# A recurrent attention block and a top-2 router on one core: buffers, order and banks around the attention stage

## The chip, the core and the metric

The kernel runs on one core of a Trainium2 chip. A core has five engines with queues of their own: TensorE (PE in the profile, with PEld for its weight loads), VectorE (DVE), ScalarE (ACT), GpSimd (POOL) and SyncE (SP), which here only issues transfers. The metric is device time in microseconds for one execution; less is better. Six runs of the kernel before gave 670.69 to 676.27 us, median 673.23 us.

## What is computed

The reference, cut to what matters. First a gated recurrence over 768 tokens for 4 batches and 8 heads of width 48, then a router that sends each of the 3072 tokens to two of eight experts.

```python
for t in range(S):                                   # S = 768
    state = f[:, :, t, :, None] * state + k_t (outer) v_t      # f = sigmoid(f_logit)
    y[:, :, t] = q_t @ state
x = y as rows of 384, one per token                  # 3072 rows
logits = x @ w_gate
noisy = logits + log1p(exp(x @ w_noise)) * noise
top2 = the two largest of noisy; weights = softmax over the two
for e in range(8):
    out[rows of e] += weight * (relu(x[rows of e] @ w1[e]) @ w2[e])
```

## The kernel before

**Stages.** The sequence is cut into chunks of 128 tokens: six per batch, so 24 chunks n = 0 to 23 (batch n % 4, group c = n // 4). The attention is a loop over steps i, in which each stage works on a chunk of its own: the sums of the log-gates run two chunks ahead of the scores, the output one behind, the features two behind. A step therefore holds work of up to six chunks. Within one step the instructions are issued in the order of the `for stage, lag in (...)` line, and `in_order` (L1222) fixes that order on every engine: nothing is reordered later, and an instruction that waits holds up everything behind it on its engine.

**One step, by engine.** TensorE: the transposes `kp` of k (L588, into PSUM bank 0), the state's share of the output `y` (L614), the scores `sc` (L599), the transposes `qp` (bank 3), `kp` (bank 1) and `fp` (bank 0), all three L555, the output `y` (L660), the state's update `ds` in two halves (L633: the first half into bank 2, the second into bank 0), the features `xp` (L670, bank 1). ScalarE: `yT` (L623), the decays `P` and `Q` (L574, L576), `far`, two passes for `f` (L560, L561), `cap`, the copy `dss` of the state's second half (L645), the copy `xs` of the x rows (L675), the copy `kn` (L593). VectorE: the scan `L` (L569), the masked scores `A` (L602), `qP` and `kQ` (L581, L583), `half` (L638), the logits' sums `lg` (L673). GpSimd: the clamp of f two chunks ahead (L549), then `mid` (L648) and the new state `st` (L649), which add and scale what `dss` holds. A state made at chunk n is first read at chunk n + 4.

**Shared results.** `lg` and `xs` read the same bank. The order of tracing decides which goes first, and the second carries a wait for the first. A bank is written again only when its last reader is done: `kp` of L588 waits for `dss` (both use bank 0), `kp` of L555 waits for the last reader of `xp` (bank 1), `xp` for `kQ` (bank 1), `ds` for the last reader of bank 2.

**The router** runs in small pieces between the stages, one group of four chunks at a time. Its last part multiplies counts on TensorE (`rk`, L734 and L735), copies them on ScalarE (`ranks`, L737), turns them into list positions on VectorE (L740 to L745), and appends each token to its experts' lists with 8 indirect transfers from GpSimd per group (`put`, L749). One put is issued for every third slot of the loop, from group 3 on for every slot.

**The weights.** The first two experts' weights are loaded in parts during the last steps (`weights_part`, L868): w1 in three parts of 128 rows, w2 in three parts of 3, 3 and 2 blocks. They are queued on SP, in its order, behind the other loads of the step. Each transfer of that queue also waits for the one eight before it. From then on TensorE works through experts; a load of weights for expert e + 2 (L864, L866) waits in SP's queue for TensorE to be done with expert e.

The last parts of expert 1 stand in SP's queue behind such a load.

Of the kernel before, what the change touches and what calls it, by code (L numbers as in the profile page):

```python
# [10 lines left out]
F32 = mybir.dt.float32  # L11
# [4 lines left out]
AX = mybir.AxisListType  # L16
ALU = mybir.AluOpType
# [314 lines left out]
def kernel(  # L332
# [38 lines left out]
    nc = tc.nc  # L371
    B, H, S, D = q.shape
    N, DM = out.shape
    E = moe_w_gate.shape[1]
    FF = moe_w1.shape[2]
    C = 128
    NCH = S // C
    HP = H // 2
    DP = 64
    KO = DM // 128  # L380
    FO = FF // 128
# [32 lines left out]
    wk = attention.enter_context(tc.tile_pool(name="wk", bufs=2))  # L414
    ps2 = attention.enter_context(tc.tile_pool(name="ps2", bufs=1, space=PSUM))
    turns = [(ps1, 3)]

    def one_bank(name, which=None):
        if which is None and len(turns) == 2 and name.startswith("xgp"):
            pool, which = turns[0]  # L420
        elif which is None or len(turns) > 2:
            turns.append(turns.pop(0))
            pool, which = turns[-1]
        else:
            pool = ps1
            if which == 3 and len(turns) == 2:
                which = 1
        return pool.tile([128, 512], F32, tag=f"bank{which}", name=name)

    def two_banks(name, tag="two"):  # L430
# [64 lines left out]
    XW = 2 * D  # L495
# [129 lines left out]
    def advance(n):  # L625
        c, b = n // B, n % B
        last = c == NCH - 1
        vt = pads["v"][n % RING["v"]]
        ds = [one_bank(f"ds{k}_{n}", 2 - 2 * k) for k in range(1 if last else 2)]
        for hp in range(HP):  # L630
            for k, par in ((0, 0), (1, 1), (0, 1), (1, 0)):
                if k < len(ds):
                    nc.tensor.matmul(ds[k][rows(par), hp * DP:(hp + 1) * DP], lhsT=kn[n][rows(k), 2 * hp + par, :],  # L633
                                     rhs=vt[rows(k), 2 * hp + par, :], start=True, stop=True)
        dsv = [t[:, 0:HP * DP].rearrange("d (a e) -> d a e", e=DP) for t in ds]
        half = wk.tile([128, HP, DP], F32, tag="half", name=f"half_{n}", bufs=3)
        if c:
            nc.vector.tensor_tensor(half, dsv[0], state[b], ALU.add)  # L638
        else:
            nc.vector.tensor_copy(half, dsv[0])  # L640
        before[n] = state[b], half
        if last:
            return
        dss = wk.tile([128, HP, DP], F32, tag="ds", name=f"dss_{n}", bufs=1)
        nc.scalar.copy(dss, dsv[1])  # L645
        new = wk.tile([128, HP, DP], F32, tag=f"st{b}", name=f"st_{n}")
        mid = wk.tile([128, HP, DP], F32, tag="mid", name=f"mid_{n}", bufs=1)
        nc.gpsimd.tensor_tensor(mid, dss, half, ALU.add)  # L648
        nc.gpsimd.tensor_tensor(new, mid, far[:, n, :].unsqueeze(2).broadcast_to((128, HP, DP)), ALU.mult)  # L649
        state[b] = new  # L650
# [15 lines left out]
    def features(n):  # L666
        c, b = n // B, n % B
        xp = one_bank(f"xp_{n}", 1)[:, 0:HP * (XW + 2 * E)].rearrange("t (a w) -> t a w", a=HP)
        for hp in range(HP):
            nc.tensor.matmul(xp[:, hp, :], lhsT=yT[n][:, hp].rearrange("e r t -> e (r t)"), rhs=w_rt[:, hp, :], start=True, stop=True)  # L670
        if b == 0:
            lg[c] = rt.tile([128, B, 2 * E], F32, tag="lg", name=f"lg_{c}", bufs=NCH)
        pace["f"] = nc.vector.tensor_reduce(lg[c][:, b, :], xp[:, :, XW:].rearrange("t a e -> t e a"), axis=AX.X, op=ALU.add)  # L673
        xs = wk.tile([128, HP, XW], F32, tag="xs", name=f"xs_{n}", bufs=3)
        nc.scalar.copy(xs, xp[:, :, 0:XW])  # L675
        xw.append(lambda: nc.sync.dma_start(out=x_rows[n * C:(n + 1) * C, :], in_=xs.rearrange("t a w -> t (a w)")))


    def route(c):
# [50 lines left out]
                                     data1=each.rearrange("t e b -> t (e b)"), initial=0.0, op0=ALU.mult, op1=ALU.add)  # L730
        for _ in range(2 if c == 0 else 5):
            yield from pause()
        rk = one_bank(f"rk_{c}", 3)[:, 0:B * E].rearrange("t (e b) -> t e b", b=B)
        nc.tensor.matmul(rk, lhsT=earlier, rhs=each[:, :, 1:], start=True, stop=False)  # L734
        nc.tensor.matmul(rk, lhsT=ones, rhs=upto[c][:, :, 0:B], start=False, stop=True)  # L735
        ranks = t([E, B], "ranks")
# [29 lines left out]
    def enough():  # L766


        total = one_bank("total_a")[:, 0:E]
        nc.tensor.matmul(total, lhsT=ones, rhs=upto[HALF - 1][:, :, B], start=True, stop=True)  # L770
        lack = rt.tile([1, E], F32, tag="lack", name="lack", bufs=1)
        nc.vector.tensor_scalar(lack, total[0:1, :], 255.5, None, ALU.is_lt)
        nc.vector.tensor_reduce(short, lack, axis=AX.X, op=ALU.max)
        yield

    def plan():


        def t(shape, tag, dtype=F32):
            return rt.tile([128] + shape, dtype, tag=f"{tag}_plan", name=f"{tag}_plan", bufs=1)  # L780

        total = one_bank("total_b")[:, 0:E]
        nc.tensor.matmul(total, lhsT=ones, rhs=upto[NCH - 1][:, :, B], start=True, stop=True)
        full, cnt, ends = t([E, NI], "full"), t([E], "cnt"), t([E], "ends")
        nc.vector.tensor_tensor(full, total.unsqueeze(2).broadcast_to((128, E, NI)),
                                over_of.unsqueeze(1).broadcast_to((128, E, NI)), ALU.is_gt)
        yield
        nc.vector.tensor_reduce(cnt, full, axis=AX.X, op=ALU.add)
        nc.vector.tensor_tensor_scan(ends, data0=ones[:, 0:E], data1=cnt, initial=0.0, op0=ALU.mult, op1=ALU.add)
        step, past, ex, row = t([E], "step"), t([NI, E], "past"), t([NI], "ex"), t([NI], "row")  # L790
        nc.vector.tensor_scalar(step, cnt, -1.0, float(N // QS), ALU.mult, ALU.add)
        yield
        nc.vector.tensor_tensor(past, block.unsqueeze(2).broadcast_to((128, NI, E)),
                                ends.unsqueeze(1).broadcast_to((128, NI, E)), ALU.is_ge)
        yield
        nc.vector.tensor_reduce(ex, past, axis=AX.X, op=ALU.add)
        nc.vector.tensor_tensor(past, past, step.unsqueeze(1).broadcast_to((128, NI, E)), ALU.mult)
        nc.vector.tensor_reduce(row, past, axis=AX.X, op=ALU.add)
        yield
        nc.vector.tensor_tensor(row, row, block, ALU.add)  # L800
        nc.vector.tensor_scalar(row, row, float(3 * 256 // QS), float(E * N // QS), ALU.add, ALU.min)
        nc.vector.tensor_scalar(ex, ex, float(E - 1), None, ALU.min)
        to = top.tile([128, NI, 2], I32, tag="steer", name="steer")
        nc.vector.tensor_scalar(to[:, :, 1], row, float(QS), None, ALU.mult)
        nc.vector.tensor_copy(to[:, :, 0], ex)
        yield
        steer_q.extend(to[0:1, n, :] for n in range(NI))
        nc.vector.tensor_scalar(more, ends[0:1, E - 1:E], NQ + 0.5, None, ALU.is_gt)
        nc.vector.scalar_tensor_tensor(short, in0=ends[0:1, E - 1:E], scalar=NI + 0.5, in1=short, op0=ALU.is_gt, op1=ALU.max)
        yield  # L810
# [56 lines left out]

    def weights_part(k, which, part):  # L868
        if which == 1:
            return nc.sync.dma_start(out=w1[k][:, part], in_=moe_w1[k, part * 128:(part + 1) * 128, :])  # L870
        else:
            few = slice((part * FO + 2) // 3, ((part + 1) * FO + 2) // 3)
            return nc.sync.dma_start(out=w2[k][:, few], in_=moe_w2[k].rearrange("(f p) d -> p f d", p=128)[:, few])

    def turned(p, s):
# [420 lines left out]
    for i in range(-3, NS + 2):  # L1296
        for stage, lag in ((summed, -2), (finish, 2), (decays, -2), (scores, 0), (scaled, -2), (forget, -3),
                           (output, 1), (advance, 0), (features, 2), (upright, -1), (upright_copy, -1)):
            n = i - lag
# [3 lines left out]
            if stage is forget:  # L1303
                clamp(n + 2, nc.gpsimd if n else nc.vector)
            elif stage is scaled:
                load("q", n + 3)
                load("k", n + 3)
                if n < 2:
                    load_router(n)
                    load("v", n + 1)  # L1310
            elif stage is finish:
                while xw:
                    xw.pop(0)()
            elif stage is scores:
                load("v", n + 3)
            elif stage is advance:
                if n in (2, 7, 8, 9, 10, 11):
                    load_router(2 + (2, 7, 8, 9, 10, 11).index(n))
                for bit in {18: (0,), 19: (1,), 20: (2, 3), 21: (4, 5), 22: (6, 7), 23: (8, 9, 10, 11)}.get(n, ()):
                    weight = weights_part(bit // 6, bit // 3 % 2 + 1, bit % 3)  # L1320
                    if n < NS - 2:
                        spaced(weight, "k")
                if n >= NS - 2:
                    zeros(HALF * B // 2)
            elif stage is upright_copy:
                load("f", i + 7)
# [24 lines left out]
        n = i - 2  # L1351
# [83 lines left out]
```

## Time and profile before

| | |
|---|---|
| six runs, median | 673.23 us |
| the profiled execution | 674.02 us |
| its span, first to last instruction | 672.3 us |
| TensorE busy | 637.5 us, 95% |
| VectorE busy | 439.6 us, 65% |
| ScalarE busy | 253.0 us, 38% |
| GpSimd busy | 273.3 us, 41% |
| mean granted TensorE clock | 0.983 |

The span falls into three stretches. Up to about 165 us is the attention with the router between; from there to about 659 us the experts; then some 13 us in which the last results are written. A window row of the profile gives, after the length of the window, the busy time of TensorE, of its weight loads, of VectorE, ScalarE and GpSimd, each with its number of instructions, then the granted clock of TensorE as a share of full speed, the busy share of the 16 DMA engines and what they moved. A row of the view of waits gives who waited for whom, the sum in us, how often, and the longest. A timeline row gives start, length, engine, line and operation; the bracket is the idle time before it and what ended it.

### The profile page before, as it was taken

What the parts mean: (1) busy time and instruction counts of PE and PEld (TensorE: products, weight loads), DVE (VectorE), ACT (ScalarE), POOL (GpSimd) and SP (SyncE); (2) the same over time, 40 slices, a digit from 0 to 9 for tenths busy, and PEclk for the clock granted to TensorE, in tenths of its full rate; (3) what the DMA queues carried; (4) which work ended last, traced back from release to release, by engine and by line L of the source; (5) the groups of instructions that cost most, each with busy time, mean ns of one, the idle gap of its engine ahead of it and who ended that gap; (6) DMA issues with size and microseconds to landing.
All of it is one profiled execution on the core that took longest, in us unless ns stands there. A gap on an engine that the chain in (4) does not pass through costs nothing.

```text
span 672.3 us, 16495 instructions
## 1 busy us (share of the span) xinstructions
PE 637.5 (95%) x6637; PEld 580.5 (86%) x6637; DVE 439.6 (65%) x1041; ACT 253.0 (38%) x597; POOL 273.3 (41%) x304
## 2 busy tenths in 40 slices
PE   6999998899999999999999999999999999999992
PEld 5788887787899999999989898898988989989891
DVE  6668776774446754445666877677876677767761
ACT  5687775662222121212243333333233232233320
POOL 8544798775066632333122424142341332502121
PEclk9999997999999999999999999999999999999997
DMA  9979798767789567662134577375872757702122
GB/s 179 193 167 210 152 193 193 170 180 272 262 246 309 195 170 233 203 175 48 12 68 111 165 271 197 112 210 154 283 188 94 223 164 269 185 25 26 21 25 28
DMA packets 159174, 110.61 MB, mean 165 GB/s; under 512 B 115104, under 2 KB 149408, under 8 KB 159088
## 3 DMA queue, kind: packets, MB, share of 16 engines
q1 hardware_dynamic: 146912, 89.91, 46.4%
q0 software_dynamic: 12176, 19.55, 13.9%
q8 instruction: 54, 0.88, 0.5%
q14 instruction: 32, 0.26, 0.1%
HBM read 88.56 MB, written 21.12 MB: 163 GB/s over the span
## 4 chain that ended last, share of the span: by engine, by line
PE 86%; ACT 4%; DVE 3%; DMA 2%; issue 1%; POOL 1%; SPq 0%; POOLq 0%; DVEq 0%; ACTq 0%
PE y L1039 31%; PE hp L931 13%; PE P L958 6%; PE W L958 4%; PE V L958 4%; PE X L958 4%; PE Z L958 4%; PE xp L670 3%; PE xgp L880 2%; PE qp L555 2%; PE y L660 2%; PE ds L633 1%; PE sc L599 1%; PE y L614 1%; PE kp L588 1%; PE kp L555 1%
## 5 line engine op out<-in xcount | busy, mean ns | idle before, releaser
L1048 POOL DMA_INDIRECT out_dram<-ys,slots x48 | 81.3, 1695 | 210.7 <-ACT ys L1105 155.2
L1039 PE MATMUL y<-qk_all,f_all 128*128 128x192 f32 x576 | 105.5, 327 | 0.0
L1039 PEld LDWEIGHTS y<-qk_all,f_all 128*128 128x128 f32 x576 | 93.5, 190 | 0.5 <-DVE xt L881 0.2
L931 PE MATMUL hp<-xt,w 128*128 128x256 f32 x384 | 86.2, 381 | 0.4 <-ACT kn L593 0.2
L931 PEld LDWEIGHTS hp<-xt,w 128*128 128x128 f32 x384 | 72.0, 190 | 9.9 <-ACT kn L593 0.4
L1039 PE MATMUL y<-w,hs 128*128 128x192 f32 x384 | 71.0, 328 | 1.0 <-DVE mid L1107 1.0
L1039 PEld LDWEIGHTS y<-w,hs 128*128 128x128 f32 x384 | 63.6, 190 | 2.4 <-DVE mid L1107 1.1
L1021 DVE TENSOR_TENSOR f_all<-hs 128x512 f32<-128x512 f32 x48 | 32.4, 689 | 40.4 <-ACT hs L933 34.9
L749 POOL DMA_INDIRECT lists<-entry,sloti x48 | 51.9, 1082 | 14.7 <-issue 8.1
L856 POOL DMA_INDIRECT xg<-x_rows,slots x48 | 50.8, 1058 | 14.5 <-issue 10.5
L933 ACT ACTIVATE hs<-hp 128x512 f32<-128x512 f32 x32 | 19.1, 597 | 73.7 <-PE hp L931 73.7
L1179 POOL DMA_INDIRECT out_dram<-ys_q,slots_q x5 | 8.6, 1716 | 80.4 <-DVE ys_q L1177 80.4
L1105 ACT ACTIVATE ys<-ys,slots 128x384 f32<-128x384 f32 x24 | 14.8, 616 | 66.4 <-DVE ys L1104 64.5
L549 POOL TENSOR_SCALAR f_all<-f_all 128x384 f32<-128x384 f32 x21 | 27.3, 1300 | 26.8 <-DMA f_all<-in_f_logit_dram 14.2
L958 PE MATMUL P<-sides,v_all 128*128 128x256 f32 x128 | 38.1, 379 | 0.0
L881 ACT COPY xt<-xgp 128x384 f32<-128x384 f32 x32 | 15.3, 478 | 57.3 <-PE xgp L880 57.3
L994 ACT ACTIVATE hs<-hs 128x256 f32<-128x256 f32 x32 | 13.4, 418 | 59.0 <-DVE hs L974 59.0
L1039 PE MATMUL y<-qk_all,hs 128*128 128x192 f32 x192 | 35.3, 327 | 0.1
L1039 PE MATMUL y<-w,f_all 128*128 128x192 f32 x192 | 35.1, 326 | 0.0
L958 PE MATMUL X<-xt,w 128*128 128x256 f32 x128 | 32.9, 379 | 0.0
L958 PE MATMUL Z<-xt,v_all 128*128 128x256 f32 x128 | 32.8, 379 | 0.0
L1097 DVE TENSOR_TENSOR ys<-P,y 128x192 f32<-128x192 f32 x24 | 8.5, 354 | 35.8 <-PE y L1039 23.1
(197 smaller groups left out, 1422.5 us busy)
## 6 DMA issues: line engine op xcount, KB each, us to landing
w<-in_moe_w_dram SPq DMA_DIRECT2D x24, 1536.0 KB
w_q<-in_moe_w_dram SPq DMA_DIRECT2D x10, 1536.0 KB
f_all<-in_f_logit_dram SPq DMA_DIRECT2D x24, 192.0 KB
qk_all<-in_q_dram SPq DMA_DIRECT2D x24, 192.0 KB
qk_all<-in_k_dram SPq DMA_DIRECT2D x24, 192.0 KB
v_all<-in_v_dram SPq DMA_DIRECT2D x24, 192.0 KB
x_rows<-xs SPq DMA_DIRECT2D x24, 192.0 KB
out_dram<-zero SPq DMA_DIRECT2D x24, 192.0 KB
```

The source lines that it names most:

```text
L549: engine.tensor_scalar(raw, raw, XMIN, None, ALU.max)
L555: nc.tensor.transpose(p[:, cols(hp)], flat[:, cols(hp)], ident)
L670: nc.tensor.matmul(xp[:, hp, :], lhsT=yT[n][:, hp].rearrange("e r t -> e (r t)"), rhs=w_rt[:, hp, :], start=True, stop=True)
L749: into = nc.gpsimd.indirect_dma_start(out=lists, out_offset=bass.IndirectOffsetOnAxis(ap=sloti[:, r, b:b + 1], axis=0), in_=entry[:, c, b, ...
L856: nc.gpsimd.indirect_dma_start(out=xg[p][:, s, :], out_offset=None, in_=x_rows[0:HALF * B * C] if p < E else x_rows, in_offset=bass.Indire ...
L881: (nc.vector.tensor_copy if p < E else nc.scalar.copy)(xt[p][:, :, s * 128:(s + 1) * 128], xp[:, 0:DM].rearrange("d (k t) -> d k t", k=KO))
L931: nc.tensor.matmul(hp[:, o, :], lhsT=w1[home(k)][:, i, (fo + o) * 128:(fo + o + 1) * 128], rhs=xt[k][:, i, :], start=(i == 0), stop=(i == ...
L933: nc.scalar.activation(hs[:, fo:fo + 2, :], hp, AF.Relu)
L958: nc.tensor.matmul(to, lhsT=x, rhs=y, start=start, stop=stop)
L1021: nc.vector.tensor_tensor(sm[which], x, y, op)
L1039: nc.tensor.matmul(P[name], lhsT=x[:, o, :], rhs=y[:, o, :], start=(o == 0), stop=(o == FH - 1))
L1048: into = nc.gpsimd.indirect_dma_start(out=out, out_offset=bass.IndirectOffsetOnAxis(ap=slots[p][:, s, 2:3], axis=0), in_=ys[s], in_offset= ...
```

## The change

- `dss` (L645) gets three buffers in place of one.
- `xs` (L675) is traced ahead of `lg` (L673): ScalarE's copy reads the bank first.
- `rk` moves from bank 3 to bank 2, the counts `total_a` and `total_b` too.
- The first two experts' weights come in eight parts each in place of six: w1 by quarters of its columns (1 KB pieces of a row in place of 4 KB rows, 384 KB a part), w2 by four equal parts (384 KB a part). They are issued at other steps: expert 0's w1 one part each at chunks 17 to 20, its w2 at 21; expert 1's w1 at 22, its w2 at 23.

Apart from the exchange of `xs` and `lg` in tracing, the order of instructions on TensorE, VectorE, ScalarE and GpSimd is the same; on SP only the weights' parts move.

```diff
@@ one_bank
             pool = ps1
-            if which == 3 and len(turns) == 2:
-                which = 1
@@ advance
-        dss = wk.tile([128, HP, DP], F32, tag="ds", name=f"dss_{n}", bufs=1)
+        dss = wk.tile([128, HP, DP], F32, tag="ds", name=f"dss_{n}", bufs=3)
@@ features
-        pace["f"] = nc.vector.tensor_reduce(lg[c][:, b, :], xp[:, :, XW:].rearrange("t a e -> t e a"), axis=AX.X, op=ALU.add)
         xs = wk.tile([128, HP, XW], F32, tag="xs", name=f"xs_{n}", bufs=3)
         nc.scalar.copy(xs, xp[:, :, 0:XW])
+        pace["f"] = nc.vector.tensor_reduce(lg[c][:, b, :], xp[:, :, XW:].rearrange("t a e -> t e a"), axis=AX.X, op=ALU.add)
@@ route
-        rk = one_bank(f"rk_{c}", 3)[:, 0:B * E].rearrange("t (e b) -> t e b", b=B)
+        rk = one_bank(f"rk_{c}", 2)[:, 0:B * E].rearrange("t (e b) -> t e b", b=B)
@@ enough, plan
-        total = one_bank("total_a")[:, 0:E]
+        total = one_bank("total_a", 2)[:, 0:E]
...
-        total = one_bank("total_b")[:, 0:E]
+        total = one_bank("total_b", 2)[:, 0:E]
@@ weights_part
         if which == 1:
-            return nc.sync.dma_start(out=w1[k][:, part], in_=moe_w1[k, part * 128:(part + 1) * 128, :])
+            few = slice(part * FF // 4, (part + 1) * FF // 4)
+            return nc.sync.dma_start(out=w1[k][:, :, few], in_=moe_w1[k].rearrange("(k p) f -> p k f", p=128)[:, :, few])
         else:
-            few = slice((part * FO + 2) // 3, ((part + 1) * FO + 2) // 3)
+            few = slice(part * FO // 4, (part + 1) * FO // 4)
             return nc.sync.dma_start(out=w2[k][:, few], in_=moe_w2[k].rearrange("(f p) d -> p f d", p=128)[:, few])
@@ the loop, stage advance
-                for bit in {18: (0,), 19: (1,), 20: (2, 3), 21: (4, 5), 22: (6, 7), 23: (8, 9, 10, 11)}.get(n, ()):
-                    weight = weights_part(bit // 6, bit // 3 % 2 + 1, bit % 3)
+                for bit in range(n - 17, n - 16) if 17 <= n < 21 else range(4 * n - 80, 4 * n - 76) if n >= 21 else ():
+                    weight = weights_part(bit // 8, bit // 4 % 2 + 1, bit % 4)
                     if n < NS - 2:
                         spaced(weight, "k")
```

## The prediction

> **What bounds the kernel now.** I read the windows first, to find where TensorE stands still or runs slowly.
>
> ```profile
> 105.00:110.00 5.00, 3.11 (x92) 2.56 (x90) 4.83 (x19) 2.77 (x8) 4.56 (x8) 1.00 0.88 192
> 110.00:115.00 5.00, 3.85 (x58) 3.41 (x59) 0.96 (x3) 3.06 (x7) 4.69 (x7) 0.55 0.94 205
> 115.00:120.00 5.00, 5.00 (x105) 4.87 (x104) 2.77 (x9) 1.92 (x6) 2.00 (x3) 0.77 0.93 203
> ...
> 130.00:135.00 5.00, 2.29 (x36) 1.94 (x40) 2.96 (x16) 1.43 (x4) 4.45 (x7) 0.94 0.74 190
> 135.00:140.00 5.00, 5.00 (x131) 4.65 (x124) 3.52 (x11) 3.57 (x10) 2.72 (x5) 0.72 0.39 83
> ```
>
> From 200 us to 650 us TensorE is busy all the time, so only the attention can give. There two places stand out: TensorE idles for over two microseconds and the clock then falls to half. Next, the view of waits over the whole span says who is late.
>
> ```profile
> ACT xs L675 <- DVE lg L673: 29.8, 21, 4.9
> ...
> ACT dss L645 <- POOL mid L648: 6.9, 4, 3.2
> ```
>
> The same view of TensorE alone, up to 200 us: its longest wait is for that copy `dss`, and two smaller ones belong to the router's `rk`.
>
> ```profile
> PE kp L588 <- ACT dss L645: 6.2, 4, 2.7
> ...
> PE rk L734 <- DVE qP L581: 1.3, 2, 1.0
> PE qp L555 <- ACT ranks L737: 1.2, 1, 1.2
> ```
>
> The timelines show the mechanism: GpSimd is a step behind with puts, `mid` of the last chunk is late, the single `dss` buffer is still being read, and ScalarE, then TensorE, stand behind it.
>
> ```profile
> 109.82 0.87 POOL L648 TENSOR_TENSOR mid<-dss,half 128x256 f32<-128x256 f32 x1
> 110.72 0.37 ACT L645 COPY dss<-ds 128x256 f32<-128x256 f32 x1 [2.87 <-POOL mid L648]
> 111.15 1.12 PE L588 MATMUL kp<-ident,kQ 128*128 128x128 f32 x4 [2.38 <-ACT dss L645]
> 117.13 0.76 PE L660 MATMUL y<-A,v_all 64*64 64x64 f32 x32
> ...
> 133.77 0.66 PE L588 MATMUL kp<-ident,kQ 128*128 128x128 f32 x4 [2.71 <-ACT dss L645]
> 138.24 0.69 PE L660 MATMUL y<-A,v_all 64*64 64x64 f32 x32
> ```
>
> And a clean step, for the margin that the new order of `xs` and `lg` uses:
>
> ```profile
> 37.57 0.23 DVE L673 TENSOR_REDUCE lg<-xp 128x16 f32<-128x64 f32 x1 [0.56 <-PE xp L670]
> 37.71 1.28 DVE L569 TENSOR_TENSOR_SCAN L<-f,cap 128x512 f32<-128x512 f32 x1
> 37.83 0.48 ACT L675 COPY xs<-xp 128x384 f32<-128x384 f32 x1 [0.85 <-DVE lg L673]
> 39.16 0.65 ACT L574 ACTIVATE P<-L 128x512 f32<-128x512 f32 x1
> 40.45 0.68 DVE L583 TENSOR_TENSOR kQ<-kp,Q 128x512 f32<-128x512 f32 x1
> 41.59 1.15 PE L670 MATMUL xp<-w_rt,yT 128*128 128x112 f32 x8
> ```
>
> **Three buffers for `dss`.** The wait for `mid` one chunk back becomes one for three chunks back. GpSimd was one step late in both places, so it is gone.
>
> *First place.* `xp` ends at 108.77; in the undisturbed step `kp` starts 0.17 before the end of `xp` (125.06 against 124.08 + 1.15), so here at 108.60 in place of 111.15: 2.55 us. From `kp` to `y` of L660 the slow clock took 117.13 - 111.15 = 5.98; the undisturbed step takes 127.91 - 125.06 = 2.85, plus 0.56 for the two `rk` (143.82 to 144.38): 3.41, so 2.57 more. Gain 5.1, if nothing else ends later.
>
> *Second place.* `xp` ends at 131.07, `kp` could start at 130.90 in place of 133.77: 2.87. Then 138.24 - 133.77 = 4.47 against 2.85: 1.62. Gain 4.5.
>
> That the slow clock follows from the idling is read from three cases: after 2.66, 2.38 and 2.71 us of idling (`kp` at 14.92, 111.15, 133.77) the windows show 0.50, after the gaps of up to 1.7 us they don't. The Trainium skill speaks against this half of the gain ("TensorE: Matmul & The Clock Gate", "HAM oscillation — how this bites in real kernels"): no idle gaps over some 3.4 us is its rule, so these gaps would not have cost the clock. By it the slow spells have another cause and stay, and 4.2 us of the sum would fall away. I go by the three rows, in which the clock drops at the gap's end.
>
> What is late next: GpSimd's clamp and `st` are still a step behind. The clamp is read two steps later, `st` four chunks later; GpSimd does 2.00 us of work in 115 to 120 and catches up. That cover is a step, some 5.3 us; without it `fp` waits.
>
> **`xs` ahead of `lg`.** ScalarE stops waiting (29.8 us in all), but it mostly waits for TensorE's `kp` right after, so this gains nothing by itself. VectorE now starts `lg` after `xs`: in the clean step at 37.54 + 0.03 + 0.48 + 0.03 = 38.08 in place of 37.57, half a microsecond later. Behind `lg` stand the scan `L`, `A`, `qP`, `kQ`; behind `kQ`, `xp`. `L` would start 0.14 after `lg` and end at 39.50, so `P` moves from 39.16 to 39.5 and `kQ` ends 0.34 later, at 41.47. `xp` starts at 41.59: the margin of 0.46 just covers it. Reading all steps so, it is not covered in three: `xp` at 64.79 starts 0.05 after `kQ` (loss 0.5), at 83.04 it is 0.25 (0.34 lost, since `P` hangs on `L` there), at 150.55 it is 0.11 (0.25). Sum: 1.1 us lost. Bounds: nothing, if ScalarE's lead helps as much; 0.5 for each of the 16 steps from 52 to 150 us, 8 us, if VectorE's routing work leaves no margin. I take 1.1, by the rows.
>
> It also shortens the two gains. In the second place `lg` starts at 131.6, `L` 0.5 later behind a maximum and its index, and the rows' lengths bring `kQ` to 136.0, `xp` to 136.05 against 139.61: 3.6 gained, not 4.5.
>
> **`rk` in bank 2.** Before, `rk` waits for `qP` (bank 3) and the next `qp` for `ranks`. Now `ds` waits for `ranks`. Group 0: `qp` no longer waits (1.17), and `ds` comes 2.2 us later, when `ranks` is long done: 1.1 gained. Groups 1 and 3: `rk` need not wait 0.96 and 0.30, but `ranks` ends at 89.20 and 145.12, where `ds` started at 89.21 and 145.13: nothing gained, nothing lost. Group 2 falls into the first place: `P` starts after `L` at 110.70, `ranks` ends 2.74 later as at 142.38 to 145.12, so at 113.45; TensorE would be at `ds` at 108.60 + 3.41 + 0.75 = 112.76. It waits 0.75: `xp` at 114.1 against 118.52, so 4.4 gained there, not 5.1. Behind the waiting `ds` stand `xp` and the whole next step. `total_a` (119.50) waits for `half` (119.14): nothing. Bounds for all groups: 1.3 gained if ScalarE is early, 3 lost if it is 0.75 late four times.
>
> **The weights.** No engine's work changes; SP issues 16 parts in place of 12, at some 0.45 us each, 1.8 us of its idle time. Expert 0's w2 now comes whole at chunk 21: 1.57 MB from 150.5 on in place of 0.98. At 357 GB/s (window 150 to 155) that takes 4.4 us in place of 2.8; its first reader is VectorE at 158.28, so some 3 us remain for the last bytes to land. If that cover went, VectorE would stand up to 4.85 us without TensorE noticing (its idle time before `A` at 165.34). Expert 1's w1 no longer stands behind the load that waits until 171.74; TensorE reads it at 188.82, so this gains nothing. The pieces shrink to 1 KB; nearest row: w2's 1.5 KB pieces and the zeros moved at 391 GB/s. Value 0; bounds: 0.9 lost (one more stop like the 0.94 us before `sc` at 153.80, where the DMA engines are full), 0.9 gained. The skill ("DMA: Bandwidth & Descriptors", "Measured (HBM→SBUF, 128 partitions, SWDGE, issued from GpSimd)") wants transfers of 1 MiB; by its fit of 2.0 us plus bytes over 436 GB/s, four parts one after another are an estimated 11.6 us, and VectorE would wait until 162, still inside its idle time.
>
> **Sum.** 4.4 + 3.6 + 1.1 - 1.1 = 8.0 us, of 674.0 us in the profiled execution: 666.0. It lies 0.8 above the median of 673.2, so the median should go to 665.2; I say 665.5, as a stop in the full DMA stretch is likelier to grow than to shrink. All experts start earlier by the same amount, and their loads hang on TensorE's progress, so nothing is given back there.
>
> **Rivals.** (a) The clock has another cause. For it: after other gaps, of up to 1.7 us, the clock stayed, so idling doesn't always cost it; against it three long gaps in three. 8.0 - 2.57 - 1.62 = 3.8 us: 669.4. (b) The loop of `xp`, `xs`, `lg`, `L`, `P`, `Q`, `kQ` becomes the bound wherever the router works: 16 steps at 0.5 take back 8 us in place of 1.1, leaving 1.1: 672.1. For it: VectorE is busy 4.83 of 5 us at 105; against it: it was late there for its own sake, `xs` was done before it came to `lg` would be, and the shift is then nothing (`lg` at 103.41, 1.4 after `xp`). (c) Slower: `ds` waits for `ranks` so long that the clock falls. Place: `ds` in groups 1 to 3; price 2.4 us of idling plus 2.1 (mean of 2.57 and 1.62), three times 13.5, against 8.0: 678.7. It decides from 2.4 us of lateness; the rows show 0 and my sum 0.75. That the wait for `mid` isn't what the profile says I hold for unlikely: ScalarE resumes within 0.05 us of its end, twice.
>
> **How the numbers follow.** Forecast 0.73, own range 661.5 to 669.5; (a) 0.08; (b) 0.11; (c) 0.08. Low end: 5.1 + 4.5 + 1.1 + 1.3 = 12 us gained and nothing lost, 661, and 0.5 for the runs' scatter; high end reaches to (b): 672. A change of 0.5% (3.4 us, to 669.9) is about what this measurement can tell from none. Faster: nearly all of the forecast and part of (a): 0.76; within: (b), the rest: 0.16; slower: 0.08.
>
> **What would show it.** After: no row of `dss` waiting for `mid` over 0.5 us; windows from 100 to 140 with the clock at 1.00; `lg` about 0.5 after `xp`; `ds` waiting for `ranks` under 1 us in group 2; `xp` of chunk 17 some 8 us earlier, and the end with it. I am wrong if a slow spell stays without a gap before it (a), if `xp` waits for `kQ` in most steps (b), or if a new gap over 2 us stands before `ds` (c).

## The result and the profile after

| | before | after |
|---|---|---|
| median of all runs beside each other | 672.47 us (51 runs) | 668.77 us (25 runs) |
| ratio, with its 95% interval | | 0.9946 (0.9933 to 0.9959) |
| the profiled execution | 674.02 us | 668.17 us |
| its span | 672.3 us | 666.4 us |
| mean granted TensorE clock | 0.983 | 0.989 |

The change gains 3.6 us, 0.54%. The interval lies wholly below 1, so it is faster, though only just by more than the 0.5% that the prediction named as about what can be told from none. The forecast was 8.0 us. The direction held and the size was under half; at 668.77 us the median still lies inside the prediction's own range of 661.5 to 669.5, 0.7 us from its slow end. The two profiled executions lie further apart than the medians, 5.9 us, since the one of before was 1.6 us slower than its median and the one after 0.6 us faster.

In the changed kernel most lines of the attention are numbered two lower (`ds` L631, `f` L558, `P` L572, `L` L567, `dss` L643, `ranks` L735); `xs` is L672 and `lg` L673. TensorE's view of waits, up to 200 us (who waited for whom, sum in us, times, longest):

```profile
PE ds L631 <- ACT f L558: 6.0, 13, 0.9
PE ds L631 <- ACT ranks L735: 3.9, 3, 1.9
PE kp L586 <- ACT f L558: 2.7, 1, 2.7
PE qp L553 <- DVE qP L579: 1.2, 1, 1.2
...
PE kp L586 <- ACT dss L643: 1.0, 2, 0.5
```

The wait for `dss`, 6.2 us with a longest of 2.7, is down to 1.0 us, and no row of `dss` waiting for `mid` is left. In its place `ds` now waits: for `ranks` 3.9 us where it was nothing, and for `f` 6.0 us, where the same view of before has

```profile
PE ds L633 <- ACT f L560: 1.8, 4, 0.7
```

Not all of this comes from the exchange; the second and third set of experiments tell more.

Of all engines, in the same stretch, the exchange of `xs` and `lg` shows thus:

```profile
ACT xs L672 <- PE xp L668: 19.2, 20, 2.9
DVE lg L673 <- ACT xs L672: 17.7, 22, 1.6
ACT P L572 <- DVE L L567: 14.4, 17, 1.7
```

ScalarE no longer waits for `lg`; VectorE waits for `xs` instead, and then ScalarE for the scan `L`, 14.4 us in 17 waits, where before had 4.0 in 3.

The windows of the two places of before, with the clock in the third column from the end, now run at full speed:

```profile
110.00:115.00 5.00, 3.68 (x138) 3.32 (x133) 3.36 (x11) 3.30 (x10) 4.92 (x7) 1.00 0.89 191
115.00:120.00 5.00, 4.47 (x122) 4.04 (x111) 3.67 (x5) 3.45 (x10) 4.32 (x7) 1.00 0.94 200
...
130.00:135.00 5.00, 4.76 (x106) 4.46 (x106) 4.86 (x12) 2.90 (x7) 4.68 (x7) 1.00 0.78 193
```

Behind them the clock is not full throughout: a period of half clock begins at 139.44 us, told below.

The next table shows where time was won and lost. It gives, at the start of `xp` of some chunks, how much earlier (minus) each trace is than the profiled execution of before. Three of the later experiments stand beside it: `dss` alone is `e9_dss`, the exchange alone `e10_swap`, `dss` and banks `e11_dss_rk`.

| `xp` of chunk | before, us | after | `dss` alone | exchange alone | `dss` and banks |
|---|---|---|---|---|---|
| 0 | 31.03 | -1.81 | -0.35 | -1.76 | -0.50 |
| 3 | 46.79 | -0.60 | -0.52 | -0.55 | -0.67 |
| 6 | 64.79 | -0.21 | -1.52 | -0.89 | -1.77 |
| 7 | 71.80 | -1.57 | -1.53 | -0.48 | -3.13 |
| 13 | 107.62 | -2.06 | -1.27 | -0.22 | -2.71 |
| 14 | 118.52 | -5.90 | -5.19 | -3.08 | -7.41 |
| 16 | 129.92 | -5.47 | -5.36 | -3.11 | -7.27 |
| 17 | 139.61 | -8.76 | -8.62 | -2.53 | -10.54 |
| 19 | 150.55 | -5.74 | -5.67 | -1.55 | -7.51 |
| 23 | 186.63 | -6.08 | -6.31 | -1.88 | -7.98 |

Take the column "after" by its steps. From chunk 13 to 14 it gains 3.8 us, from 16 to 17 3.3: these are the two stops behind `dss`. At chunk 7 it gains 1.4: group 0's `qp` no longer waits for `ranks`. Two losses stand against that: 1.2 us between chunks 0 and 3, where no router works, and 3.0 us between 17 and 19. (The 1.8 us at chunk 0 are no part of the change: before, the clock fell after the gap at 14.9 us; here the same gap, 2.65 us, left it alone. More on this in the last section.) The five steps sum to 3.8 + 3.3 + 1.4 - 1.2 - 3.0 = 4.3 us, and with the 1.8 of chunk 0 they are the 6.1 us at chunk 23. From chunk 20 on nothing changes any more.

**The first loss, a clean step.** The timelines of ScalarE, VectorE and TensorE in the changed kernel (start, length, engine, line, operation, bracket with the idle time before it and its releaser):

```profile
36.09 0.48 ACT L672 COPY xs<-xp 128x384 f32<-128x384 f32 x1 [0.60 <-PE xp L668]
...
36.60 0.23 DVE L673 TENSOR_REDUCE lg<-xp 128x16 f32<-128x64 f32 x1 [1.09 <-ACT xs L672]
36.74 1.49 DVE L567 TENSOR_TENSOR_SCAN L<-f,cap 128x512 f32<-128x512 f32 x1
...
38.27 0.63 ACT L572 ACTIVATE P<-L 128x512 f32<-128x512 f32 x1 [0.67 <-DVE L L567]
...
39.41 0.59 ACT L558 ACTIVATE f<-fp 128x512 f32<-128x512 f32 x1
...
40.05 0.69 PE L631 MATMUL ds<-v_all,kn 64*64 64x64 f32 x30 [0.40 <-ACT f L558]
```

The same place before:

```profile
40.31 0.61 ACT L560 ACTIVATE f<-fp 128x512 f32<-128x512 f32 x1
...
40.97 0.69 PE L633 MATMUL ds<-v_all,kn 64*64 64x64 f32 x30
```

The exchange makes `lg` wait for `xs`, so the scan `L` starts half a microsecond later. ScalarE gets to `P` and stands 0.67 us for `L`. Behind `P` in ScalarE's order are `Q`, `far` and then the first pass of `f`, which reads `fp` in bank 0. The second half of `ds` writes bank 0, so TensorE stands 0.40 us for `f`. Before, `f` ended at 40.92 and `ds` followed without a wait.

**The second loss, group 3 of the router.** The same timelines, a hundred microseconds later:

```profile
133.34 0.19 DVE L673 TENSOR_REDUCE lg<-xp 128x16 f32<-128x64 f32 x1
133.46 1.63 DVE L567 TENSOR_TENSOR_SCAN L<-f,cap 128x512 f32<-128x512 f32 x1
...
135.12 0.63 ACT L572 ACTIVATE P<-L 128x512 f32<-128x512 f32 x1 [1.57 <-DVE L L567]
...
137.65 0.18 ACT L735 COPY ranks<-rk 128x32 f32<-128x32 f32 x1
...
137.88 0.68 PE L631 MATMUL ds<-v_all,kn 64*64 64x64 f32 x16 [1.90 <-ACT ranks L735]
```

VectorE comes late to `lg` because of its routing work. `P` waits 1.57 us for `L`, both passes of `f` and then `ranks` follow, and the first half of `ds`, which now shares bank 2 with `rk`, stands for 1.90 us. After that the clock is at half for a while, though the gap is shorter than all those that cost the clock before. Windows of the changed kernel, cut where the clock changes (last columns: granted clock, DMA share, GB/s):

```profile
136.03:139.44 3.41, 1.56 (x24) 1.50 (x25) 2.23 (x7) 1.73 (x6) 1.50 (x3) 1.00 0.43 97
139.44:142.85 3.41, 3.41 (x60) 2.88 (x60) 1.97 (x4) 2.50 (x5) 2.80 (x3) 0.50 1.05 243
142.85:146.27 3.42, 3.42 (x82) 3.06 (x80) 1.82 (x4) 0.57 (x3) 2.70 (x3) 1.00 0.95 316
```

Half clock for 3.41 us costs up to 1.7 us of work; with the wait of 1.90 that covers the 3.0 us of the table. In another execution of the changed kernel (`e8_after`) a wait of 1.88 us at the same place was not followed by half clock, and 2.0 us were lost between chunks 17 and 19.

### The profile page after: what moved, and what is told of

Read it like the earlier page. It is cut to its first block, busy times and chain, and to the rows that moved or that the text cites. A ratio compares the mean times of both kernels' runs of the same rounds, so it can differ in the third digit from the quotient of the medians.

```text
span 666.4 us, 16496 instructions
## 1 busy us (share of the span) xinstructions
PE 633.9 (95%) x6637; PEld 577.4 (87%) x6637; DVE 441.4 (66%) x1041; ACT 254.7 (38%) x597; POOL 272.0 (41%) x304
## 4 chain that ended last, share of the span: by engine, by line
PE 80%; ACT 5%; DVE 5%; DMA 4%; issue 2%; POOL 2%; SPq 1%; POOLq 0%; DVEq 0%; ACTq 0%
PE y L1038 32%; PE hp L930 13%; PE P L957 7%; PE W L957 4%; PE Z L957 4%; PE V L957 4%; PE X L957 4%; DVE L L567 3%; PE xp L668 3%; PE xgp L879 2%; PE ds L631 1%; ACT f L558 1%; ACT P L572 1%; PE yp_q L1172 1%; PE hp_q L1157 1%
## 5 line engine op out<-in xcount | busy, mean ns | idle before, releaser
L1047 POOL DMA_INDIRECT out_dram<-ys,slots x48 | 79.8, 1663 | 208.7 <-ACT ys L1104 158.2
L547 POOL TENSOR_SCALAR f_all<-f_all 128x384 f32<-128x384 f32 x21 | 24.8, 1181 | 27.8 <-DMA f_all<-in_f_logit_dram 19.9
L567 DVE TENSOR_TENSOR_SCAN L<-f,cap 128x512 f32<-128x512 f32 x24 | 32.2, 1343 | 1.5 <-ACT cap L562 1.5
```

The lines of the kernel that those rows point to most:

```text
L547: engine.tensor_scalar(raw, raw, XMIN, None, ALU.max)
L567: nc.vector.tensor_tensor_scan(L[n], data0=logf[n], data1=cap[n % 2].rearrange("d a t -> d (a t)"), initial=0.0, op0=ALU.add, op1=ALU.min)
L1047: into = nc.gpsimd.indirect_dma_start(out=out, out_offset=bass.IndirectOffsetOnAxis(ap=slots[p][:, s, 2:3], axis=0), in_=ys[s], in_offset= ...
```

## The experiments

Two theories at the start. A: the stops behind `dss` are worth about what the prediction reckoned, and the reordering gave part of it back. B: the stops were covered by other work, and there was little to gain. The kernels of one set ran on one chip; each ratio is against the kernel before in the same set.

**First set: each part alone.** `e1_dss` is the kernel before with `bufs=3`, `e2_swap` with `xs` and `lg` exchanged, `e3_rk` with the ranks and totals in bank 2, `e4_weights` with the weights in eight parts; in each case these lines of the change and no others.

> Before, with three buffers for dss and nothing else. Theory A (the two buffer stops were worth what the prediction says; the other order of xs and lg and the ranks' new bank gave part of it back): both stops and both slow spells go, 5.1 + 4.5 us by the rows of before, less a little that comes up behind them; 7 to 9.5 us faster, ratio 0.986 to 0.990. Theory B (the stops were covered by other work: VectorE's and GpSimd's queues set the pace there once the buffer no longer does): the same 3.6 us as the whole change or less, ratio 0.994 or above.

> Before, with only xs traced ahead of lg. Theory A: P hangs on L in nearly all steps, so both passes of f come later and the second half of ds, which writes f's bank, waits for them: the waits of ds for f grow from 1.8 us (4 times) to about 6 us (13 times); 2 to 4 us slower, ratio 1.003 to 1.006. Theory B: the margins cover it, within 1 us of before, ratio 0.9985 to 1.0015.

> Before, with only the ranks and the totals in bank 2. Theory A: 1.2 us gained in group 0, and ds waits for ranks in groups 1 to 3, 0.7 to 1.9 us each, with a slow spell where it is 1.9: 0 to 3 us slower, ratio 1.000 to 1.005. Theory B: only the group 0 gain counts, ratio 0.998.

> Before, with only the weights in eight parts at the new steps. Both theories: VectorE waits some 2 us for expert 0's w2 and TensorE does not notice: ratio 0.9985 to 1.0015. If the denser transfers stop TensorE's instructions (as in the one stop of 0.94 us that the profile of before puts down to nothing), up to 1 us slower.

Measured: 698.72 us, ratio 1.0033 (1.0006 to 1.0059); 697.96 us, 1.0015 (0.9992 to 1.0039); 698.95 us, 1.0009 (0.9982 to 1.0035); 699.09 us, 1.0028 (1.0007 to 1.005). On this chip the kernel before itself took 697.57 us, some 25 us more than in the runs above. None of the four is faster; `e1_dss` and `e4_weights` are 0.3% slower, with intervals clear of 1. By the numbers B would stand, but the traces show that something else held TensorE up here. TensorE's waits up to 200 us with `dss` in three buffers:

```profile
PE y L614 <- issue: 7.8, 15, 1.1
PE ds L633 <- issue: 7.1, 14, 1.1
```

and a window of it:

```profile
120.00:140.00 20.00, 16.02 (x340) 13.39 (x343) 8.72 (x19) 9.70 (x26) 15.41 (x23) 0.83 0.45 97
```

"issue" means that TensorE waited for nothing that the profile shows. It idled 14.9 us this way ahead of the small matmuls of `y` and `ds`, the clock was at 0.83, and the stretch went slowly whatever the other engines did. The other three traces have such rows too. The four runs say nothing on A or B where these gaps are absent, and the same questions were put again.

**Second set: the change with one part undone.** The kernel before took 670.91 us here. `e8_after` is the changed kernel itself. `e5_no_swap` undoes the exchange alone:

```diff
+        pace["f"] = nc.vector.tensor_reduce(lg[c][:, b, :], ...)
         xs = wk.tile([128, HP, XW], F32, tag="xs", name=f"xs_{n}", bufs=3)
         nc.scalar.copy(xs, xp[:, :, 0:XW])
-        pace["f"] = nc.vector.tensor_reduce(lg[c][:, b, :], ...)
```

`e6_no_rk` puts ranks and totals back where they were before. `e7_dss_rk0` is the kernel before with three buffers for `dss` and `one_bank(f"rk_{c}", 3 if c else 2)`: bank 2 for group 0 only.

> The changed kernel itself, so that all of this call stand beside it on one chip. Theories A and B: ratio 0.993 to 0.996 to before as in the result. Theory C, where the gaps fill the steps: 1.000 to 1.004.

> After, with lg traced ahead of xs again (so: three buffers, ranks in bank 2, eight parts). Theory A (half of the gain was given back by the new order of xs and lg and by the ranks): 2 to 3 us faster than the changed kernel of this call; the waits of ds for f fall from 6.0 us (13 times) to 2 us or less. Theory B (the removed stops were covered by other work): as the changed kernel, within 1 us, whatever the waits of ds say. Theory C (the four runs before this: TensorE there stood 0.3 to 0.5 us at a time before small matmuls of the state without anything to wait for, from about 85 to 180 us, and the step was set by that): where such gaps fill the steps, no edit shows, and all kernels of this call lie within 0.4% of before.

> After, with the ranks in bank 3 and the totals by turns again. Theory A: the waits of ds for ranks (3.9 us, 3 times, and a slow spell behind the one of 1.9) go, the wait of qp for ranks in group 0 (1.2 us) comes back, and rk waits again for qP: 1 to 3 us faster than the changed kernel. Theory B: as the changed kernel. Theory C: within 0.4% of before.

> Before, with three buffers for dss and the ranks in bank 2 for group 0 alone; order of xs and lg, the other banks and the weights as before. Theory A: 9 to 10.5 us faster than before, ratio 0.985 to 0.988, the fastest of this call. Theory B: 0.994. Theory C: within 0.4% of before.

Measured: `e8_after` 667.69 us, 0.995 (0.9926 to 0.9974); `e5_no_swap` 664.3 us, 0.9904 (0.9868 to 0.9939); `e6_no_rk` 671.87 us, 1.0021 (0.9998 to 1.0045); `e7_dss_rk0` 664.53 us, 0.9909 (0.9878 to 0.9941).

The change repeats its gain in this set. Without the exchange it is 3.4 us faster, where A had 2 to 3. The waits of `ds` for `f` fall from 4.7 us (`e8_after`) to 2.8, not to the 2 that A named, and those for `ranks` from 4.0 to 2.8: 3.1 us together, about the gain. So A is right that the exchange gives part back, and the rest of both waits is there without it. `e7_dss_rk0` gains 6.4 us, less than the 9 to 10.5 of A. About the ranks A is wrong. It took their move for one of the steps that gave something back; undone, the kernel is 4.2 us slower, not faster. TensorE's waits in `e6_no_rk`:

```profile
PE ds L633 <- ACT f L560: 5.2, 13, 0.7
PE rk L734 <- DVE qP L581: 3.5, 3, 1.7
```

With the ranks in bank 3 `rk` waits for `qP`, 3.5 us where before had 1.3. The exchange isn't needed for this wait: `e9_dss` below, with the old order, has 3.2 us of it, and `e10_swap`, the exchange without the buffers, only 1.6. The wait of `qp` for `ranks` in group 0 is back as well, 1.5 us, and the trace, like that of the changed kernel, has a period of half clock at 139 us. Without the exchange, bank 2 for all groups (`e5_no_swap`) and for group 0 alone (`e7_dss_rk0`) come to the same. So the new bank is worth 4.2 us beside the exchange and, by the third set, some 0.6 without it. Why so much more is not shown.

**Third set: the parts alone again, and a better order.** The kernel before took 670.75 us. `e9_dss` and `e10_swap` are `e1_dss` and `e2_swap` again. `e11_dss_rk` has the three buffers and the new banks, with the old order of `lg` and `xs` and the old parts of the weights. `e12_ranks_early` is `e11_dss_rk` with one more edit in the router, which puts `rk` ahead of `fp` on TensorE and so `ranks` ahead of both passes of `f` on ScalarE:

```diff
-        for _ in range(2 if c == 0 else 5):
+        for _ in range(2 if c == 0 else 4):
             yield from pause()
         rk = one_bank(f"rk_{c}", 2)[:, 0:B * E]...
```

> The kernel before with three buffers for dss and nothing else. Theory A: the two stops behind dss are worth about what the prediction gave them (8.0 us together, some of it given back to waits that were hidden behind them, so 5 to 7.5 us); the ratio is 0.989 to 0.993 and no wait of kp for dss is left in TensorE's waits above 1 us. Rival B: most of the gain needs the ranks in another bank too; the ratio is 0.994 to 0.998 and waits of rk for qP take over. If TensorE shows gaps behind nothing on this chip that slow it everywhere, as on the chip of the first look, all four lie within 0.4% of before.

> The kernel before with only the order of xs and lg exchanged. Theory A: the later logits make P and with it both passes of f later, so ds waits for f; the exchange alone costs 3 to 6 us, a ratio of 1.004 to 1.009, with waits of ds for f above 3 us in sum in the first 200 us. Rival B (the prediction's own step: it costs 1.1 us): within 0.2% of before, and no more waits of ds for f than the 1.8 us of before.

> The changed kernel without the exchange of xs and lg and with the weights in four parts: three buffers for dss, ranks in the other bank. Both theories: the parts of the weights are worth nothing, so as the run without the exchange alone, a ratio of 0.989 to 0.992. If eight parts matter, it is 0.994 or above, or below 0.987.

> As the run before it, with the matmul of the ranks and ScalarE's copy of them put one place earlier, ahead of both passes of f instead of between them. Theory A: what is left of waits of ds for ranks (2.8 us in three waits without the exchange) goes, and the passes of f come 0.3 us later in three steps; 1 to 2 us better than the run before it, a ratio of 0.986 to 0.990. Rival B: the wait moves to rk itself, for qP or for the sums before it, or to ds for f; no better than the run before it, within 0.2%.

| | median, us | ratio | interval |
|---|---|---|---|
| `e9_dss` | 665.82 | 0.9927 | 0.9913 to 0.994 |
| `e10_swap` | 674.3 | 1.0062 | 1.0045 to 1.008 |
| `e11_dss_rk` | 665.3 | 0.9918 | 0.9901 to 0.9934 |
| `e12_ranks_early` | 664.01 | 0.9904 | 0.9889 to 0.9919 |

One edited number, `bufs=3`, gains 4.9 us, by the medians more than the whole change. The exchange alone costs 0.62%, 4.2 us by the ratio (3.6 by the medians), and its trace shows the wait that A named:

```profile
PE kp L588 <- ACT dss L645: 5.0, 4, 2.0
PE ds L633 <- ACT f L560: 4.4, 12, 0.7
```

Rival B, the prediction's own 1.1 us, would be a ratio of 1.0016 and lies below the interval. The profiled execution of `e10_swap` was its fastest, and at chunk 23 it stands ahead of that of before, so the whole cost comes from the medians and can't be read in the table. Part of the loss can: from chunk 0 to 3 the exchange alone loses 1.2 us, exactly as the changed kernel does, and the two columns without it lose nothing. The other traces of these two sets agree: 1.1 and 1.3 us lost in the two with the exchange (`e8_after`, `e6_no_rk`), nothing in the three without it.

In `e9_dss` the gain of the two places is 3.9 and 3.3 us in the table, and then 3.0 us are given back between chunks 17 and 19. There `rk` waits, and the clock falls again. Two rows of TensorE's waits and one of its timeline:

```profile
PE ds L633 <- ACT f L560: 4.0, 9, 1.0
PE rk L734 <- DVE qP L581: 3.2, 3, 1.2
...
136.65 0.41 PE L734 MATMUL rk<-each,earlier 128*128 128x32 f32 x2 [1.22 <-DVE qP L581]
```

So the buffers alone also make `ds` wait more for `f` than the 1.8 us of before. And part of what is removed at 133 us comes back at 137, with either bank for `rk`: `e11_dss_rk` gives 3.0 us back there too, with a period of half clock as here, `e5_no_swap` and `e7_dss_rk0` 1.5 us without one, in the one execution of each that was profiled.

The eight parts of the weights are the only difference of `e5_no_swap` to `e11_dss_rk`: 0.9904 against 0.9918, intervals that overlap widely, on different chips. No effect was found here. In the first set the eight parts alone were 0.28% slower, and the buffers alone, which gain 0.73% here, 0.33% slower.

`e12_ranks_early` is the fastest at 0.96% under before, and 1.3 us under `e11_dss_rk`; the intervals of the two overlap, so that last step is likely, not shown. It is faster than the kernel before, as are `e5_no_swap`, `e7_dss_rk0`, `e9_dss` and `e11_dss_rk`. All five have a lower ratio than the changed kernel, but only `e5_no_swap` and `e7_dss_rk0` ran beside it, 3.4 and 3.2 us under it. Its trace shows the wait for `ranks` gone and why not more came of it. TensorE's waits:

```profile
PE fp L553 <- POOL f_all L547: 3.2, 2, 2.7
PE kp L586 <- ACT f L558: 2.6, 1, 2.6
PE ds L631 <- ACT f L558: 2.6, 7, 0.5
```

and the timeline of GpSimd and TensorE:

```profile
122.48 1.35 POOL L747 DMA_INDIRECT lists<-entry,sloti  x1 [0.22 <-issue]
...
124.14 0.96 POOL L747 DMA_INDIRECT lists<-entry,sloti  x1 [0.22 <-issue]
...
125.16 1.19 POOL L547 TENSOR_SCALAR f_all<-f_all 128x384 f32<-128x384 f32 x1
...
126.40 1.11 PE L553 MATMUL fp<-ident,f_all 128*128 128x128 f32 x4 [2.75 <-POOL f_all L547]
```

With the ranks early, the puts are early too, and TensorE is further ahead: at chunk 14 this kernel is 10.0 us before the kernel before, against 7.4 for `e11_dss_rk`. Then the clamp of `f_all` stands behind five puts in a row, TensorE waits 2.75 us for it, the clock falls, and at chunk 17 it is 9.9 against 10.5. (Of its lead in these traces 1.3 us stand at chunk 0 already, ahead of the router, and are no part of the edit.) Spreading these puts was not tried.

## Why the prediction was right and wrong

**What bounds the kernel, and the two places.** Right about what stops TensorE there. Reckoned net gains were 4.4 and 3.6 us; the trace after shows 3.8 and 3.3. The second came out near partly by luck. The prediction took 0.9 us off 4.5 for the later `lg`, but the traces without the exchange (`e5_no_swap`, `e7_dss_rk0`, `e9_dss`, `e11_dss_rk`) gain the same 3.3. In each of them, and in the changed kernel, `ds` waits 0.93 to 0.96 us for `f` in that step, which may be what is missing. In the first place `e5_no_swap`, `e7_dss_rk0` and `e11_dss_rk` gain 4.7 to 4.8 us, `e9_dss` 3.9, since `rk` waits 1.19 us for `qP` there. Once won, the time stayed won through the experts: 6.1 us at chunk 23, with the 1.8 us that the change did not make, and 5.9 in the span.

**The clock.** That the half clock comes from TensorE's idling was right, and rival (a) fell: with the stops gone, both places ran at 1.00 in the trace after. The rows were misread in one point: the clock did not drop at the gaps' ends but at 110.50 us, 0.65 ahead of the end of one, and at 134.39, 0.62 behind the end of the other. That a gap of up to 1.7 us is harmless and one of 2.4 is not was wrong as a rule, and rival (c) was priced by it. Gaps of 1.22 (`e9_dss`), 1.35 (`e11_dss_rk`) and 1.90 us (after) were followed by half clock, one of 2.65 us (after, at 14.7) was not. The last section shows what goes with it instead.

**`xs` ahead of `lg`: the step that failed.** The prediction followed the later `lg` through `L`, `P`, `qP` and `kQ` to `xp`, found a margin of 0.46 us there, and counted 1.1 us in three steps. In the changed kernel `xp` indeed waits for `kQ` only 0.2 us. But `P`, which the prediction had moved from 39.16 to 39.5, is also ahead of `Q`, `far` and `f` on ScalarE, and `ds` waits for `f` through bank 0, with no margin: `f` ended at 40.92 before, `ds` started at 40.97. The chain that decided ran through the engine's order and a shared bank, not through the data. Cost measured: 3.4 us (change against `e5_no_swap`) to 4.2 us (`e10_swap`), in place of 1.1. The path is shown by the waits and by the early steps that lose with the exchange and not without it; that the whole cost runs along it is not. Rival (b) charged 0.5 us for every step with router work, 8 us in sum, and looked for it at `xp`; the cost lies about halfway between it and the forecast, stands at `ds`, and begins in steps without router work.

**The ranks.** Group 0 was right: 1.1 reckoned, 1.4 in the trace. Group 2 waits 1.32 us where 0.75 was reckoned. Group 3 was put at nothing and waits 1.90 us, and the clock went with it: 3.0 us. The reckoning there used `ranks` and `ds` of before, where `ranks` ended as `ds` started, though the stops that hold TensorE back ahead of this place were to go. By the traces less than a third of the wait is the exchange's: without it `e5_no_swap` and `e11_dss_rk` wait 1.34 and 1.35 us at this place. There too both passes of `f` stand ahead of `ranks`; with `ranks` put ahead of them (`e12_ranks_early`) the wait is gone. Rival (c) named this place, asked for 2.4 us of lateness three times, and got one of three at 1.9. As a sum the bank still pays in this kernel: in bank 3 `rk` waits in its place, and the kernel is 4.2 us slower (`e6_no_rk`).

**The weights.** Nothing that the third set could tell, as reckoned; the 0.28% of the first set stands against it, on the chip with the unexplained gaps.

**The sum.** 4.4 + 3.6 + 1.1 - 1.1 = 8.0. By the runs, `dss` alone is worth 4.9 after what it gives back at 137 us, the banks some 0.6 (`e11_dss_rk` against `e9_dss`, within the intervals), the exchange costs 3.4 to 4.2. The ratio of `dss` and banks, 0.9918, with the 0.0062 of the exchange alone would be 0.998; the change has 0.995. The parts don't add up: the bank gains far more beside the exchange than without it, which the prediction did not have and no run explains. So it is partly luck that the median fell inside the stated range: by the parts alone it would have lain outside.

## What to carry to other kernels

When an instruction is moved or delayed, follow the order of every engine that it sits on, and every bank that the late instructions hold, not only the data: the wait came out several instructions later, at a matmul that shares no data and no bank with the two that were exchanged. An order that shortens the waits of an engine which is not the bound (ScalarE's 29.8 us for `lg`) may lengthen those of the one that is. When several edits come together, run each alone and each undone: the best one here was worth more alone than with its companions, and another was worth 4.2 us beside a third and next to nothing without it.

## What the runs showed of the hardware

**The clock changes in periods of 3.41 us.** The ten traces of the result, the second and the third set hold thirteen spells of half clock between 9 and 165 us. All lasted 3.41 or 6.83 us. Those of one execution lie on one grid: before, they begin at 14.92, 110.50 and 134.39 us, which are 28.0 and 7.0 periods apart. Windows of the kernel before on that grid:

```profile
107.09:110.50 3.41, 1.68 (x38) 1.43 (x38) 2.95 (x11) 0.73 (x2) 3.02 (x6) 1.00 0.71 141
110.50:113.91 3.41, 2.76 (x53) 2.32 (x54) 0.09 (x1) 2.28 (x5) 3.17 (x6) 0.50 1.03 235
113.91:117.33 3.42, 3.42 (x24) 3.35 (x27) 1.99 (x3) 1.53 (x5) 2.33 (x3) 0.50 0.87 196
117.33:120.74 3.41, 3.41 (x127) 3.17 (x127) 2.19 (x9) 1.91 (x6) 1.34 (x2) 1.00 0.81 160
```

The clock is exactly 0.50 or 1.00 in each. Counted by whole periods on such grids from 7 to 165 us: of 9 periods at full clock in which TensorE was busy under 48%, 8 were followed by half clock; of 24 with 48 to 65%, 5; of 405 with more, none. So it is the idle share of a period that goes with the clock, rather than the length of a gap, and where the grid lies differs from execution to execution. The changed kernel was profiled twice. At 137.88 above the gap of 1.90 us lay almost whole within one period, 46% busy, and half clock followed. In `e8_after` the same wait reads

```profile
137.34 0.68 PE L631 MATMUL ds<-v_all,kn 64*64 64x64 f32 x16 [1.88 <-ACT ranks L735]
```

Its grid, read from the drop at 655.12 us as the run ends, cuts this gap in two, and the clock stays:

```profile
132.88:136.30 3.42, 2.58 (x64) 2.41 (x63) 3.30 (x6) 1.86 (x5) 2.73 (x3) 1.00 0.29 40
136.30:139.71 3.41, 2.19 (x28) 1.89 (x28) 1.49 (x7) 1.50 (x6) 2.50 (x3) 1.00 0.86 238
139.71:143.12 3.41, 3.19 (x122) 2.93 (x122) 3.27 (x5) 2.17 (x5) 2.70 (x3) 1.00 1.05 314
```

The share alone doesn't decide either. `e7_dss_rk0` and `e9_dss` both have a gap of 1.22 us before `rk`, whole within one period that is busy for 2.19 us. First the two windows of `e7_dss_rk0`, then those of `e9_dss`:

```profile
131.34:134.75 3.41, 2.19 (x64) 1.84 (x64) 2.51 (x5) 3.08 (x8) 1.65 (x2) 1.00 0.11 7
134.75:138.17 3.42, 3.42 (x87) 3.08 (x80) 2.79 (x8) 1.56 (x4) 2.12 (x2) 1.00 0.82 209
...
135.19:138.60 3.41, 2.19 (x72) 1.84 (x69) 2.41 (x6) 2.64 (x7) 2.79 (x4) 1.00 0.91 236
138.60:142.02 3.42, 3.42 (x35) 3.05 (x38) 2.08 (x5) 1.06 (x2) 2.50 (x4) 0.50 1.04 304
```

What sets them apart stays open. Between chunks 17 and 19 the executions with the spell lost 1.0 us (`after` against `e8_after`) to 1.6 us (`e11_dss_rk` against `e5_no_swap`) more than those without it. That is likely part of the scatter of the runs, and a reason to go by medians. The Trainium skill says on the page that the prediction named ("TensorE: Matmul & The Clock Gate", "What's actually happening") that activity is judged in a free-running window of 3413 ns; the spells and their grid agree with that. Its other section, which the prediction drew on, allows gaps up to some 3.4 us; these traces don't agree: gaps from 1.22 us on were followed by half clock, in periods that were busy for up to 64%.

**In the first set the kernel was 4% slower**, 697.57 against 670.75 to 672.47 us, with idle time on TensorE that the profile puts down to nothing. That set ran on another chip than the second and the third; whether the chip is the cause stays open, since nothing was run there again. There the change could not be judged.
